# Weight pieces of a delta-rule kernel released at other moments, and step 1's scaled values computed on another engine

## The chip, the cores and the metric

The kernel runs on one core of a Trainium2 chip. Its time is the device time of one execution in microseconds (us). The engines are named as in the profile: PE (TensorE, with PEld for its weight loads), DVE (VectorE), ACT (ScalarE), POOL (GpSimd) and SP (SyncE, which issues most DMAs here).

## The reference

A delta-rule attention over 4 batches, 8 heads, 768 tokens of 48 dimensions, then a feed-forward block with a leaky slope per hidden unit; all in fp32.

```python
k_n = k / (np.linalg.norm(k, axis=-1, keepdims=True) + 1e-06)
for t in range(S):
    kt, vt, bt = (k_n[:, :, t], v[:, :, t], beta[:, :, t, None])
    y[:, :, t] = np.einsum('bhd,bhde->bhe', q[:, :, t], state)
    v_old = np.einsum('bhde,bhd->bhe', state, kt)
    state = state + bt[:, :, :, None] * np.einsum('bhd,bhe->bhde', kt, vt - v_old)
x = y.transpose(0, 2, 1, 3).reshape(B * S, H * D)      # 3072 x 384
h = x @ w_in                                           # 384 x 2048
g = np.maximum(h, 0.0) + alpha * np.minimum(h, 0.0)
out = g @ w_out                                        # 2048 x 384
```

## The kernel before

The sequence is cut into 12 chunks of 64 tokens, and each chunk into two steps of two batches (steps 0 to 23, two batches in the two halves of the partitions). Within a chunk the recurrence becomes a triangular system, which is solved with block inverses. The outputs of a chunk's two steps are transposed into `xt`, and the feed-forward block of that chunk (`ffn_in`, line 1075, then `ffn_out`) is woven between the attention matmuls of later steps. The whole schedule is written out by hand: the order of the program's text is the order on each engine's queue.

The start has a path of its own. `first_chunk` solves steps 0 and 1 together: DVE places the inverses (`place_small`, line 706), PE makes `matrix` and `own_values` for both steps, then three `rounds` follow (`one_round`, lines 857 and 912), whose third gives `u`. Then come `outputs` and `to_ffn`. `second_pair` does the same for steps 2 and 3 with pieces of `ffn_in(0)` in between (`alongside`). `scale_first` (line 845) multiplies a step's values by the norms of its keys: three products, for step 0 on POOL and for step 1 on DVE in `first_chunk`.

`busy` issues matmuls whose result nobody reads, between the start's real ones.

The weights arrive as raw 64-bit words (twice the bytes) and are converted in the kernel: `weights` handles them in pieces. A piece is fetched by one DMA on SP into a staging place (line 223), then ACT makes two passes (lines 240 and 242), DVE shifts (line 256), and POOL or DVE adds (line 263). `w_in` has 12 pieces of 512 KB and `w_out` 16 pieces of 384 KB; they are numbered from 0. The ids of a piece name its staging place; a place may be filled again once the piece in it was added. The staging places of `w_out`'s pieces 3 to 6 lie in the part of `w_out` itself that is filled last, which is free by then.

A DMA waits on SP, and with it everything behind it on SP, until the last writer and readers of its destination are done. `pause(n, upto)` (line 1671) writes one element of a staging place by a memset on POOL ahead of the fetch, so that the fetch can't start before POOL has come that far. Before the change it stands for `w_in`'s piece 4 (line 1671, ahead of the three rounds) and for piece 5 (in `second_pair`), and `pause_out` (line 1683) for `w_out`'s pieces 0 and 1. `w_out`'s pieces 3 and 4 are fetched in `second_pair` by `fetch_out(4)` and `fetch_out(5)`, and then one more piece behind each finished addition (the last argument of `weights`, `pace`, is 1). The additions of `w_out`'s first five pieces are on POOL, the others on DVE.

## Time and profile before

| | |
|---|---|
| three runs | 652.60, 651.75, 646.87 us; median 651.75 |
| the profiled execution | 648.95 us, of which the span from the first to the last instruction is 647.2 |
| mean granted clock of PE | 0.997 |
| PE / PEld busy | 635.0 / 562.7 us (98% / 87% of the span) |
| DVE / ACT / POOL busy | 482.9 / 258.6 / 125.3 us |
| DMA | 36.89 MB, of 106,799 packets 99,872 under 512 B |
| SP's wait for the memsets at line 1671 | 16.6 us in two waits |

The page has one row for each group of instructions with the same line, engine and tiles. In a timeline a row is a run of equal instructions: start in us from the span's start, how long they took, engine and line, what was written from what, shapes, count, and in brackets the idle time before them with what ended it. A row that names "issue" tells of time in which the engine waited for nothing that the profile shows. "SPq" rows are DMAs issued by SP; how long a transfer took to land is told apart from it.

### The profile page before, as it was taken

What the parts mean: (1) busy time and instruction counts of PE and PEld (TensorE: products, weight loads), DVE (VectorE), ACT (ScalarE), POOL (GpSimd) and SP (SyncE); (2) the same over time, 40 slices, a digit from 0 to 9 for tenths busy, and PEclk for the clock granted to TensorE, in tenths of its full rate; (3) what the DMA queues carried; (4) which work ended last, traced back from release to release, by engine and by line L of the source; (5) the groups of instructions that cost most, each with busy time, mean ns of one, the idle gap of its engine ahead of it and who ended that gap; (6) DMA issues with size and microseconds to landing.
All of it is one profiled execution on the core that took longest, in us unless ns stands there. A gap on an engine that the chain in (4) does not pass through costs nothing.

```text
span 647.2 us, 21391 instructions
## 1 busy us (share of the span) xinstructions
PE 635.0 (98%) x9177; PEld 562.7 (87%) x9177; DVE 482.9 (75%) x1160; ACT 258.6 (40%) x605; POOL 125.3 (19%) x248
## 2 busy tenths in 40 slices
PE   8899999999999999999999999999999999999997
PEld 7677787567889989989989989989999999999997
DVE  5858689978998788578678577678868568477383
ACT  6667664245553253254154144034045054042240
POOL 7267610010001000000000010000044053062360
PEclk9989999999999999999999999999999999999999
DMA  8668755113511320311210211211221210100000
GB/s 131 169 160 240 208 129 129 23 29 64 99 25 29 76 50 3 69 37 23 60 27 17 46 32 26 41 40 22 43 42 19 54 23 2 39 2 3 25 0 26
DMA packets 106799, 36.89 MB, mean 57 GB/s; under 512 B 99872, under 2 KB 103088, under 8 KB 106704
## 3 DMA queue, kind: packets, MB, share of 16 engines
q1 hardware_dynamic: 104832, 35.03, 25.0%
q8 instruction: 72, 1.18, 0.8%
q10 hardware_dynamic: 1872, 0.49, 0.4%
q14 instruction: 23, 0.19, 0.1%
HBM read 30.78 MB, written 4.72 MB: 55 GB/s over the span
## 4 chain that ended last, share of the span: by engine, by line
PE 86%; DVE 8%; issue 2%; ACT 2%; POOL 1%; DMA 1%; SPq 0%; POOLq 0%; DVEq 0%; ACTq 0%
PE p_ffn L1075 24%; PE p_ffn L1140 17%; PE p_more L1392 8%; PE p_more L1308 5%; PE p_ffn L1118 4%; PE p_ffn L1298 3%; PE p_ffn L1392 3%; PE p_ffn L1303 2%; PE p_pair L430 2%; PE p_pair L807 2%; PE p_pair L747 2%; PE p_pair L486 2%; PE p_pair L930 2%; PE p_pair L917 2%; PE p_pair L795 1%
## 5 line engine op out<-in xcount | busy, mean ns | idle before, releaser
L1075 PE MATMUL p_ffn<-xt,w_in 128*128 128x256 f32 x768 | 177.5, 384 | 0.7 <-DVE act L1087 0.5
L1075 PEld LDWEIGHTS p_ffn<-xt,w_in 128*128 128x128 f32 x768 | 142.0, 190 | 21.5 <-issue 1.5
L1085 ACT ACTIVATE act<-p_ffn 128x512 f32<-128x512 f32 x56 | 33.3, 595 | 80.4 <-PE p_ffn L1075 80.2
L1087 DVE SCALAR_TENSOR_TENSOR act<-act,al_t,p_ffn 128x256 f32<-128x256 f32 x112 | 48.5, 474 | 20.0 <-ACT act L1085 19.7
L1332 POOL TENSOR_TENSOR k_t<-k_t 128x128 f32<-128x128 f32 (+1 forms) x48 | 29.9, 623 | 167.5 <-ACT k_t L1327 165.0
L571 DVE TENSOR_TENSOR block<-block,prod 128x30 f32<-128x30 f32 (+9 forms) x150 | 50.0, 333 | 5.2
L565 DVE TENSOR_TENSOR prod<-block 128x30 f32<-128x30 f32 (+9 forms) x150 | 49.0, 327 | 4.2 <-POOL block L555 2.7
L419 POOL TENSOR_TENSOR beta_t<-beta_t,rec 128x8 f32<-128x8 f32 x20 | 5.1, 257 | 235.2 <-DVE rec L413 219.3
L1140 PE MATMUL p_ffn<-w_out,act 128*128 128x192 f32 x288 | 49.6, 328 | 0.0
L973 ACT COPY xt<-p_pair 128x384 f32<-128x384 f32 x22 | 10.4, 478 | 91.2 <-PE p_pair L969 77.5
L1140 PEld LDWEIGHTS p_ffn<-w_out,act 128*128 128x128 f32 x288 | 46.6, 190 | 0.3
L1332 POOL TENSOR_TENSOR block<-block 128x128 f32<-128x128 f32 (+1 forms) x48 | 28.0, 583 | 16.0 <-ACT block L1327 13.5
L1298 PE MATMUL p_ffn<-xt,w_in 128*128 128x256 f32 x96 | 28.7, 381 | 0.5 <-DVE o_sb L1160 0.5
L759 ACT COPY inv<-p_pair 32x256 f32<-32x256 f32 x40 | 14.5, 361 | 24.9 <-DVE u L921 24.1
L1160 DVE TENSOR_TENSOR o_sb<-u,p_ffn 128x192 f32<-128x192 f32 x24 | 7.9, 351 | 20.5 <-PE p_ffn L1140 20.0
L799 ACT COPY y<-p_pair 128x384 f32<-128x384 f32 x22 | 10.5, 479 | 31.1 <-PE p_pair L795 29.5
L1346 DVE SCALAR_TENSOR_TENSOR act<-block,al_t,act 128x256 f32<-128x256 f32 x32 | 19.1, 638 | 4.7 <-ACT block L1342 4.7
L1327 ACT COPY k_t<-p_more 128x512 f32<-128x512 f32 x16 | 9.4, 587 | 31.7 <-PE p_more L1308 27.9
L825 DVE TENSOR_TENSOR r<-v_raw,p_pair 64x192 f32<-64x192 f32 (+1 forms) x60 | 21.2, 353 | 1.0
L1392 PE MATMUL p_more<-w_out,act 128*128 128x192 f32 x128 | 21.9, 329 | 0.0
L1118 PE MATMUL p_ffn<-w_out,act 128*128 128x384 f32 x64 | 21.7, 490 | 0.0
L921 DVE TENSOR_TENSOR u<-p_pair,wgt 128x384 f32<-128x384 f32 x20 | 11.1, 555 | 14.0 <-PE p_pair L747 14.0
(286 smaller groups left out, 1424.1 us busy)
## 6 DMA issues: line engine op xcount, KB each, us to landing
v_raw<-in_v_dram SPq DMA_DIRECT2D x48, 96.0 KB, 3.1
qp<-in_q_dram SPq DMA_DIRECT2D x48, 96.0 KB, 3.1
out_dram<-o_sb SPq DMA_DIRECT2D x90, 48.0 KB, 1.6
space_out<-in_moe_w_out_dram SPq DMA_DIRECT2D x11, 384.0 KB, 4.0
ke<-in_k_dram SPq DMA_DIRECT2D x43, 96.0 KB, 3.4
kl<-in_k_dram SPq DMA_DIRECT2D x80, 48.0 KB, 2.7
w_out<-in_moe_w_in_dram SPq DMA_DIRECT2D x6, 512.0 KB, 5.1
w_out<-in_moe_w_out_dram SPq DMA_DIRECT2D x5, 384.0 KB, 5.9
```

The source lines that it names most:

```text
L565: nc.vector.tensor_tensor(out=prod, in0=r[:, 0:j, j : j + 1].to_broadcast([128, j, n]), in1=r[:, j : j + 1, j + 1 : HB].to_broadcast([128, ...
L571: nc.vector.tensor_tensor(out=r[:, 0:j, j + 1 : HB], in0=r[:, 0:j, j + 1 : HB], in1=prod, op=ALU.add)
L825: nc.vector.tensor_tensor(out=r[to, a], in0=v_in[to, a], in1=p[own, a, :, 0:D], op=ALU.subtract)
L1075: nc.tensor.matmul(p_h[:, i], w_in[:, t, (f + i) * 128 : (f + i + 1) * 128], xt[:, t], start=(t == 0), stop=(t == KT - 1),)
L1085: nc.scalar.activation(g, p_h, ACT.Relu, scale=-1.0)
L1087: nc.vector.scalar_tensor_tensor(out=g[:, i], in0=g[:, i], scalar=al_t[:, f + i : f + i + 1], in1=p_h[:, i], op0=ALU.mult, op1=ALU.add,)
L1118: nc.tensor.matmul(p_o[u], gs[f // 2][:, f % 2, u * 128 : (u + 1) * 128], w_out[:, f], start=(f == 0), stop=(f == FT - 1),)
L1140: nc.tensor.matmul(p, x(i), w(i), start=(i == 0), stop=(i == FP - 1))
L1298: nc.tensor.matmul(p[:, f * 256 : f * 256 + 256], w(2, f), xt[:, 2], start=True, stop=False)
L1308: nc.tensor.matmul(q[:, j], a, b, start=True, stop=True)
L1332: nc.gpsimd.tensor_tensor(out=dst, in0=a, in1=b, op=ALU.add)
L1392: nc.tensor.matmul(p, x(i), w(i), start=(i == 0), stop=(i == FP - 1))
```

## The change

Four edits. The values of step 1 are scaled by `scale_by_head`, twelve products on ACT, one for each head and half (128x48 or 64x48), four of them behind `slopes()` and eight ahead of `eliminate_small`; the three products on DVE in `first_chunk` go, and the last `busy` in front grows from 1.2 to 1.8 matmuls of 512 columns. In `first_chunk` the shift of `w_in`'s piece 1 stands between the two additions of the third round and its addition right behind them; `pause` for piece 4 stands behind that instead of ahead of the rounds. In `weights`, where there is a pace, each fetch behind an addition is preceded by a one-element memset into its staging place on the engine of that addition. In `second_pair`, `fetch_out(4)` becomes `pause_out(3, 4)`, and `fetch_out(5)` goes, so that piece 4 and all later ones are fetched one behind each addition, at first one addition later than before. In the built program the order of the DMAs on SP and of the matmuls on PE stays the same.

```diff
@@ weights, finish
                 while n < last and ids[n] not in ids[i + 1 : n]:
+                    if pace:
+                        engine.memset(stages[ids[n]][0:1, 0:1].bitcast(FP32), 0.0)
                     n += 1
                     fetch(n)
@@
+    def scale_by_head(n, which):
+
+        if n not in rhs_:
+            rhs_[n] = work.tile([128, 2, G, D], FP32, name="r")
+        x = v_raw[n].rearrange("p (g a) d -> p a g d", a=2)
+        w = stats[n][0].rearrange("p (g a) -> p a g", a=2)
+        for a, to, own in which:
+            for g in range(G):
+                nc.scalar.mul(rhs_[n][to, a, g], x[own, a, g], w[own, a, g : g + 1])
@@ first_chunk
         turn_matrix(0, nc.scalar)
-        scale_first(1, nc.vector)
         z_0 = own(0)
@@ first_chunk
         for n in both:
             mask(n)
+        for i in range(2):
+            rounds(i)
+        for x in [one_round(n, 2, ps_big()[:, :, 0:WY]) for n in both]:
+            now(x)
+            convert(1)
         pause(STAGED, STAGED + 1)
-        for i in range(3):
-            rounds(i)
-        convert(1)
         y_0 = outputs(0, ps_big()[:, :, 0:WY])
         now(y_0)
         begin_in()
-        convert(2)
+        convert(1)
         now(outputs(1, ps_big()[:, :, 0:WY]))
@@ the start
     slopes()
+    scale_by_head(1, [(0, slice(0, 128), slice(0, 128))])
     busy(3.2, ffn_banks[0])
@@ the start
-    busy(1.2, big[1][:, 0])
+    scale_by_head(1, [(1, half(0), half(1)), (1, half(1), half(0))])
+    v_raw.pop(1)
+    busy(1.8, big[1][:, 0])
     eliminate_small()
@@ second_pair
         alongside(2, 2)
-        fetch_out(4)
+        pause_out(3, 4)
         burst(lambda i, p: one_round(i, 1, p), G * D)
@@ second_pair
         burst(lambda i, p: one_round(i, 2, p), G * D)
-        fetch_out(5)
         alongside(3, 3, (part(blocks, 2), 2))
```

## The prediction

> **What bounds the kernel now.** I read the page first, then busy time by stage, then the timeline of each engine around the edits. On the page TensorE (PE) is busy for 98% of the span.

> ```profile
> span 647.2 us, 21391 instructions
> PE 635.0 (98%) x9177; PEld 562.7 (87%) x9177; DVE 482.9 (75%) x1160; ACT 258.6 (40%) x605; POOL 125.3 (19%) x248
> ...
> q8 instruction: 72, 1.18, 0.8%
> ```

> All edits act before 115 us. Busy time by stage (after the stretch: its length, then PE, PEld, DVE, ACT, POOL busy, clock, DMA share, GB/s) tells what there is to win:

> ```profile
> 26.97:33.68 6.71, 6.01 (x313) 5.34 (x313) 5.47 (x12) 5.44 (x12) 4.37 (x5) 1.00 0.05 16
> 33.68:34.67 0.99, 0.00 (x1) 0.00 (x1) 0.00 (x0) 0.55 (x1) 0.23 (x2) 1.00 0.00 0
> 34.67:38.34 3.67, 3.67 (x78) 3.13 (x78) 2.51 (x6) 1.53 (x3) 2.17 (x2) 0.54 0.54 147
> ...
> 60.00:69.25 9.25, 9.21 (x218) 7.09 (x211) 6.67 (x18) 5.33 (x12) 8.58 (x15) 1.00 0.96 270
> 69.25:70.23 0.98, 0.00 (x0) 0.00 (x0) 0.13 (x1) 0.00 (x0) 0.86 (x3) 1.00 1.02 389
> ...
> 80.00:105.00 25.00, 24.93 (x238) 20.74 (x237) 21.30 (x60) 14.20 (x33) 4.16 (x10) 1.00 0.60 140
> ```

> Until 34 us a serial chain runs (place the inverses, rounds); from 38 us PE is the bound. Two holes of 1 us stand out, at 33.68 and 69.25, and a stretch at clock 0.54. Both holes are "issue", PE waiting for nothing that the profile shows. Queue q8 moved 1.18 MB, which over PE's 18,354 instructions is 64 B each; its packets are 16 KB, so one holds 256 instructions, 128 pairs of load and matmul. The holes lie 765 matmuls apart, six times 127.5. I read them as PE running out of instructions. The trace's q8 packet for the first hole started at 31.70, 1.3 us after the count passed the boundary before (30.43), in an idle DMA; for the second it started at 67.97, 3.4 us after (64.60), in a DMA share of 0.96.

> ```profile
> 27.43 1.10 DVE L845 TENSOR_TENSOR r<-v_raw,first_norm 128x192 f32<-128x192 f32 x3
> 27.73 0.59 ACT L884 COPY act<-p_pair 128x512 f32<-128x512 f32 x1 [2.40 <-PE p_pair L857]
> 28.56 0.56 DVE L895 COPY act<-p_pair 128x384 f32<-128x384 f32 x1
> 35.19 0.56 DVE L912 TENSOR_TENSOR u<-act,p_pair 128x384 f32<-128x384 f32 x1 [1.70 <-PE p_pair L857]
> 36.16 3.21 POOL L263 TENSOR_TENSOR w_in<-w_out,w_in 128x512 uint32<-128x512 uint32 x2 [2.25 <-DVE w_out L256]
> 39.32 0.09 POOL L1671 MEMSET w_out<- 1x1 f32 x1
> ```

> **Part 1: step 1's values on ACT.** Three DVE products (1.10 us) leave. They stood between the inverses and the copy at 28.56, whose matmuls (started 27.48, 0.63 us) end at 28.11: DVE gains 0.4, the rest was hidden. The order of the built program puts twelve ACT products in. Nearest rows: 64x80 at 231 ns, 128x16 at 218, 64x16 at 180, 128x128 at 396; 48 columns lie near the first two, so 0.23 each. Four (0.9 us; bounds 0.7 to 1.6) fall into ACT's 1.60 us idle before 20.88; eight (1.8; 1.4 to 3.2) into the 2.40 before 27.73. Without that cover, or at the upper bound, 0.8 of it delays the copy at 27.73. The filler grows by 0.6 of 512 columns: 3.2 of them took 3.04 us, so 0.6 us within PE's 1.25 us wait before 26.97. **-0.4 us** (-0.5 to +0.4).

> **Part 2: a shift between two additions, fifth piece later.** The shift (L256, 0.4 us) enters the 1.70 us that DVE waits for the stalled matmuls before 35.19, so it costs nothing; without that wait, 0.4. POOL's two 1.6 us additions started at 36.16 because both shifts came after the second u; now the first starts when POOL is free of the masks (33.88) and ends near 35.2, the second near 37.4. The fifth w_in piece is released by a memset behind the first addition: 35.3 instead of 33.94. It took 3.8 us to land, so 39.1; ACT first reads it at 39.39. Nothing, with 0.3 us to spare. The sixth piece, at the head of a DMA stream that is saturated to 58 us, is released behind the second addition: 37.5 instead of 39.44. ACT waits for that stream (2.69 us idle before 43.89), but PE idles only 0.65 us in 50 to 60. **-0.3 us** (0 to -0.7).

> **Part 3: w_out's pieces one at a time.** Thirteen one-element memsets enter, each behind an addition, each holding one DMA: six on POOL (0.09 each by L1671), seven on DVE (0.06 by L279). DVE has 3.7 us idle from 80 to 105, which covers its 0.4. The SP order stays, but each held DMA now holds the queue. Pieces 3, 4, 5 (from 0) were issued at 64.28, 64.94, 65.43 and landed in 4.2 to 6.4 us, under each other; now they wait for POOL's additions that end at 67.74, 69.16, 71.18. A piece alone lands in 3.2 us, so at 71.0, 72.5, 74.5; ACT reads them at 72.39, 73.43, 74.49. Their traffic leaves the time in which PE's instructions were late, so I drop most of the hole:

> ```profile
> 70.23 0.56 PE L857 MATMUL p_pair<-r,sums 64*64 64x48 f32 x24 [0.98 <-issue]
> ```

> **-0.9** (0 to -1.0). PE then arrives 0.9 earlier and piece 5 is that much late for ACT; behind it wait the xt copies and the next Relu. Most fits into ACT's gaps: **+0.2** (0 to +1.2).

> [...]

> The dear place is later. Piece 9 was released by an addition on POOL, and SP issued it at 74.87; now it waits for the addition of piece 5 on DVE (82.79 to 83.3). Behind it on SP stand ten loads and piece 10:

> ```profile
> 74.87 0.33 SPq L223 DMA_DIRECT2D space_out<-in_moe_w_out_dram  x1
> 75.25 2.59 SPq L175 DMA_DIRECT2D kl<-in_k_dram  x4
> 77.88 1.43 SPq L137 DMA_DIRECT2D qp<-in_q_dram  x2
> 79.35 2.88 SPq L137 DMA_DIRECT2D v_raw<-in_v_dram  x4
> 86.14 0.34 SPq L223 DMA_DIRECT2D w_out<-in_moe_w_out_dram  x1
> ...
> 89.99 0.56 ACT L240 ACTIVATE w_out<-w_out 128x384 uint32<-128x384 uint32 x1
> 91.25 0.60 ACT L1085 ACTIVATE sums<-p_ffn 128x512 f32<-128x512 f32 x1 [0.70 <-PE p_ffn L1075]
> ...
> 95.37 0.60 ACT L1085 ACTIVATE sums<-p_ffn 128x512 f32<-128x512 f32 x1 [2.15 <-PE p_ffn L1075]
> ```

> In the times of before: memset 83.4, plus 0.35 + 2.59 + 1.43 + 2.88, gives piece 10 at 90.7 instead of 86.14. Rows near it landed in 3.3 to 4.6 us: 94.0 to 95.3, where ACT wants it at 89.99. ACT blocks, with the Relu of 91.25 behind it. That runs 0.55 later, then 0.60, then two DVE slopes (0.87): the bank is free at 96.0 to 97.3. PE fills the other bank until 95.3, so it stalls 0.7 to 2.0; near the middle, **+1.4** (0 to +2.0). By piece 13 SP has caught up (97.4 against 97.77), so it happens once.

> **Sum.** -0.4 - 0.3 - 0.9 + 0.2 + 1.4 = 0.0 against the profiled execution's own 648.95 us (span 647.2). The three runs had a median of 651.75, 2.8 above it. I forecast the middle of the two, **650.3 us**: no change.

> **Rivals.**
> *Slower: piece 10 is later still* (0.25). It decides once piece 10 lands after 93.3 (95.3 less 0.55, 0.60, 0.87). In the saturated stretch w_in pieces took 6.9 to 9.3 us; the ten loads just ahead speak for that, the DMA share of 0.60 against. Landing at 97.6 to 100.0 stalls PE 4.3 to 6.7 instead of 1.4: 653.2 to 655.6.
> *The pacing buys nothing* (0.15): earlier transfers and ke loads alone make the instructions late, the hole stays; the hole at 33.68 in an idle DMA speaks for it. 0.9 more: 651.2.
> *The clock* (0.15). From 34.69 the clock was 0.50 for 3.4 us, after a stretch with gaps. A longer filler might avoid it. Full-speed rows (outputs 1.08 us at 72.29 against 2.08 here, transposes 0.66 against 1.41) price it at -1.7: 648.6. Against: the hole at 33.68 stays. [...]

> **How the numbers follow.** The forecast holds 0.45. Nearly all of it, and most of the rivals, lie within 1% (6.5 us), about what a measurement of this kernel can tell from no change: the holes and the slow clock together are below 4 us. Faster by over 1% has 0.08, from the clock and a run that starts low (646.87); slower 0.15, from a stall at the far end with more behind it; same 0.77. The range goes from 646.0 (clock won and no stall make 647.2, less 1.2 for a low run) to 656.5 (the stall at its far end, 655.6, and the hole still there).

> **What would show it.** Right: the copy at 28.56 comes 0.4 earlier; the sixth piece is issued near 37.5; no hole near 69; SP issues piece 10 some 4 us later, and ACT waits for it with PE idle for 1 to 2 us near 95. Wrong: no wait of ACT there, or the holes as long as before, or a wait at 72 to 77 that stops PE.

## The result, and the profile after

The changed kernel took 655.02 us (median of 18 runs, 650.80 to 657.62), the kernel before 647.63 (18 runs, 645.93 to 652.60). The ratio is 1.009 (95% interval 1.0065 to 1.0115): by it the change makes the kernel 5.8 us slower (the two medians are 7.4 apart), where 650.3 and "no change" were forecast. Costs below go by the ratio.

The first lines of the page after stand beside those of before: a span of 655.9 us instead of 647.2, with the same work on PE and the same 1.18 MB of instructions.

```profile
span 655.9 us, 21415 instructions
PE 635.4 (97%) x9177; PEld 561.5 (86%) x9177; DVE 483.6 (74%) x1164; ACT 261.5 (40%) x617; POOL 124.7 (19%) x254
...
q8 instruction: 72, 1.18, 0.7%
```

PE's order is the same in both kernels, so the start of the same matmul tells where time was lost. Matmuls are counted from the start of the program; times are from the two profiled executions (that of after, 657.62 us, is the longest of its 18 runs, so it shows more loss than the median):

| matmul | before, us | after, us | after minus before |
|---|---|---|---|
| 400 | 28.82 | 28.87 | 0.0 |
| 892 | 48.40 | 49.86 | +1.5 |
| 1000 | 53.95 | 58.19 | +4.2 |
| 1200 | 62.97 | 67.78 | +4.8 |
| 1365 | 70.25 | 73.63 | +3.4 |
| 1490 | 79.57 | 84.23 | +4.7 |
| 1650 | 95.38 | 102.65 | +7.3 |
| 1700 | 100.09 | 108.86 | +8.8 |
| 9170 | 642.48 | 651.19 | +8.7 |

Two places hold nearly all of it: 42 to 61 us, where w_in's pieces arrive, and 95 to 107 us, where w_out's pieces 10 to 12 do. Behind matmul 1700 nothing changes any more.

The first place, in busy time by stage (after the stretch: its length, then PE, PEld, DVE, ACT, POOL busy, clock, DMA share, GB/s), with the stretch that answers to 80 to 105 of before as the last:

```profile
26.69:33.68 6.99, 5.68 (x314) 5.13 (x313) 4.25 (x10) 6.63 (x17) 4.58 (x5) 1.00 0.15 59
33.68:34.62 0.94, 0.23 (x17) 0.16 (x8) 0.36 (x2) 0.59 (x1) 0.50 (x1) 1.00 0.00 0
...
53.38:56.40 3.02, 0.21 (x11) 0.08 (x3) 1.10 (x3) 2.02 (x4) 0.52 (x2) 1.00 0.97 299
57.44:60.85 3.41, 3.41 (x69) 2.58 (x68) 2.16 (x6) 2.53 (x5) 2.41 (x4) 0.50 0.07 19
...
82.00:107.30 25.30, 20.68 (x213) 16.20 (x211) 17.95 (x53) 13.50 (x30) 3.54 (x8) 1.00 0.67 156
```

The start, with its hole at 33.68, is as it was. A hole of 3 us stands at 53.38, in a DMA share of 0.97, and 1 us behind it PE runs for 3.41 us at half its clock. The kernel before has no hole at these matmuls; its PE timeline has all 32 in one row:

```profile
52.11 0.85 PE L486 MATMUL p_pair<-k_t 48*64 48x64 f32 x32
```

In the last stretch PE is busy for 20.7 of 25.3 us, where it was busy for 24.93 of 25.

The timeline of POOL and of PE shows the release of the two w_in pieces (the memsets, L1684) and that the 3 us hole is "issue" (a row gives the idle time from the modelled end of the last matmul, 0.2 us less than from its start):

```profile
34.12 1.31 POOL L263 TENSOR_TENSOR w_in<-w_out,w_in 128x512 uint32<-128x512 uint32 x1 [0.82 <-DVE w_out L256]
35.36 0.09 POOL L1684 MEMSET w_out<- 1x1 f32 x1
35.97 1.29 POOL L263 TENSOR_TENSOR w_in<-w_out,w_in 128x512 uint32<-128x512 uint32 x1 [0.52 <-DVE w_out L256]
37.21 0.09 POOL L1684 MEMSET w_out<- 1x1 f32 x1
...
56.40 0.46 PE L488 MATMUL p_pair<-k_t 48*64 48x64 f32 x14 [2.81 <-issue]
```

The second place, first on SP. Piece 9 (the last of the three at 80.52, issued at 88.30) holds ten loads and piece 10:

```profile
80.52 8.10 SPq L223 DMA_DIRECT2D space_out<-in_moe_w_out_dram  x3
88.68 2.59 SPq L175 DMA_DIRECT2D kl<-in_k_dram  x4
91.32 1.29 SPq L137 DMA_DIRECT2D qp<-in_q_dram  x2
92.65 2.66 SPq L137 DMA_DIRECT2D v_raw<-in_v_dram  x4
95.43 0.56 SPq L223 DMA_DIRECT2D w_out<-in_moe_w_out_dram  x1
...
97.46 1.04 SPq L223 DMA_DIRECT2D space_out<-in_moe_w_out_dram  x2
```

Then on ACT, which waits for pieces 10 and 11, and on PE, which waits behind that for a bank (ffn_in is L1087 here, the Relu L1097):

```profile
100.28 0.55 ACT L240 ACTIVATE w_out<-w_out 128x384 uint32<-128x384 uint32 x1 [5.25 <-DMA w_out<-in_moe_w_out_dram]
100.73 0.58 ACT L1097 ACTIVATE sums<-p_ffn 128x512 f32<-128x512 f32 x1
...
103.46 0.56 ACT L240 ACTIVATE w_out<-space_out 128x384 uint32<-128x384 uint32 x1 [1.71 <-DMA space_out<-in_moe_w_out_dram]
```

```profile
83.39 0.67 PE L1087 MATMUL p_ffn<-xt,w_in 128*128 128x256 f32 x2 [0.72 <-ACT act L1097]
...
102.36 2.83 PE L1087 MATMUL p_ffn<-xt,w_in 128*128 128x256 f32 x12 [2.09 <-DVE sums L1099]
107.27 1.10 PE L1087 MATMUL p_ffn<-xt,w_in 128*128 128x256 f32 x4 [1.46 <-DVE sums L1099]
```

### The profile page after: what moved, and what is told of

Its sections match the earlier page's. It is cut to its first block, busy times and chain, and to the rows that moved or that the text cites. A ratio compares the mean times of both kernels' runs of the same rounds, so it can differ in the third digit from the quotient of the medians.

```text
span 655.9 us, 21415 instructions
## 1 busy us (share of the span) xinstructions
PE 635.4 (97%) x9177; PEld 561.5 (86%) x9177; DVE 483.6 (74%) x1164; ACT 261.5 (40%) x617; POOL 124.7 (19%) x254
## 3 DMA queue, kind: packets, MB, share of 16 engines
q8 instruction: 72, 1.18, 0.7%
## 4 chain that ended last, share of the span: by engine, by line
PE 84%; DVE 7%; ACT 2%; DMA 2%; issue 2%; SPq 1%; POOL 1%; ACTq 0%; DVEq 0%; POOLq 0%
PE p_ffn L1087 21%; PE p_ffn L1152 17%; PE p_more L1404 8%; PE p_more L1320 5%; PE p_ffn L1130 4%; PE p_ffn L1310 3%; PE p_ffn L1404 3%; PE p_ffn L1315 2%; PE p_pair L809 2%; PE p_pair L432 2%; PE p_pair L749 2%; PE p_pair L942 2%; PE p_pair L929 2%; PE p_pair L797 1%; PE p_pair L488 1%
## 5 line engine op out<-in xcount | busy, mean ns | idle before, releaser
L1087 PE MATMUL p_ffn<-xt,w_in 128*128 128x256 f32 x768 | 178.7, 385 | 5.2 <-DVE sums L1099 3.9
L1087 PEld LDWEIGHTS p_ffn<-xt,w_in 128*128 128x128 f32 x768 | 142.1, 190 | 26.8 <-ACT w_out L242 2.5
L1097 ACT ACTIVATE act<-p_ffn 128x512 f32<-128x512 f32 x56 | 33.3, 595 | 82.5 <-PE p_ffn L1087 82.2
L985 ACT COPY xt<-p_pair 128x384 f32<-128x384 f32 x22 | 10.4, 477 | 90.7 <-PE p_pair L981 76.9
L809 PE MATMUL p_pair<-beside,k_t 48*64 48x112 f32 x704 | 21.7, 259 | 1.1 <-issue 0.9
L966 DVE TENSOR_TENSOR beside<-beside,p_pair 48x384 f32<-48x384 f32 (+1 forms) x38 | 20.8, 549 | 2.1 <-PE p_pair L958 1.9
```

Of the source, the lines that this page charges most:

```text
L809: nc.tensor.matmul(p[half(t ^ a), a, g], k_t[n][dims(a), g, half(t)], beside[bp][dims(a), t, g])
L1087: nc.tensor.matmul(p_h[:, i], w_in[:, t, (f + i) * 128 : (f + i + 1) * 128], xt[:, t], start=(t == 0), stop=(t == KT - 1),)
L1097: nc.scalar.activation(g, p_h, ACT.Relu, scale=-1.0)
```

## The experiments

Each was timed beside the kernel before; the ratio is to that. Two more, `pages_moved` and `extra_traffic`, ran once each (653.94 and 650.66 us), for their profiles.

| kernel | median, us | before, us | ratio (95%) |
|---|---|---|---|
| only_scale | 647.58 | 647.66 | 0.9999 (0.9985 to 1.0014) |
| only_rounds | 649.50 | 647.66 | 1.0029 (1.0005 to 1.0052) |
| only_pace | 651.53 | 647.66 | 1.0063 (1.0046 to 1.0080) |
| nine_early | 650.54 | 647.66 | 1.0039 (1.0011 to 1.0067) |
| pace_memsets | 651.85 | 647.65 | 1.0061 (1.0046 to 1.0076) |
| shift_alone | 647.95 | 647.65 | 0.9999 (0.9981 to 1.0016) |
| fifth_alone | 649.30 | 647.65 | 1.0024 (1.0008 to 1.0040) |
| sixth_held | 647.65 | 647.65 | 1.0002 (0.9990 to 1.0013) |
| pace_nine | 647.65 | 647.42 | 1.0001 (0.9985 to 1.0017) |
| mended | 651.05 | 647.42 | 1.0060 (1.0039 to 1.0080) |
| no_scale | 649.01 | 647.80 | 1.0021 (1.0005 to 1.0037) |
| no_pacing | 648.48 | 647.80 | 1.0013 (0.9997 to 1.0028) |
| scale_pace | 649.79 | 647.80 | 1.0027 (1.0013 to 1.0042) |
| fifth_back | 647.21 | 647.80 | 1.0005 (0.9983 to 1.0027) |

### The parts by themselves

`only_scale` is the kernel before with step 1's values on ACT:

```diff
-        scale_first(1, nc.vector)
+    scale_by_head(1, [(0, slice(0, 128), slice(0, 128))])
     busy(3.2, ffn_banks[0])
...
-    busy(1.2, big[1][:, 0])
+    scale_by_head(1, [(1, half(0), half(1)), (1, half(1), half(0))])
+    busy(1.8, big[1][:, 0])
```

> Before, with step 1's values on ACT and the longer filler alone. Theory: the loss sits in the other two parts, so this lies within 0.2% of before, 0 to 0.4 us faster, with the copy of the first values some 0.4 us earlier. Rival: the early microseconds move the hand-off between PE and its instruction fetches for the whole start, and this alone is 3 us or more slower.

It changes nothing, as expected: the copy of the first values does come 0.4 us earlier (28.14 instead of 28.56). The hole at 69 us, which the prediction priced, is not in its profile though every release of a piece is as before: it is not there in every execution.

`only_rounds` is the kernel before with the shift between the additions and the fifth piece behind the last round:

```diff
-        pause(STAGED, STAGED + 1)
-        for i in range(3):
+        for i in range(2):
             rounds(i)
-        convert(1)
+        for x in [one_round(n, 2, ps_big()[:, :, 0:WY]) for n in both]:
+            now(x)
+            convert(1)
+        pause(STAGED, STAGED + 1)
...
-        convert(2)
+        convert(1)
```

> Before, with the shift between two additions and the fifth w_in piece behind the last round alone. Theory: the saturated stream of w_in pieces starts some 2 us earlier, PE's instruction packets come later in it, and PE has holes of 1 to 3 us between 47 and 58 us at matmul counts 853 and 981: 3 to 5 us slower. Rival: those holes in the profile of the changed kernel were chance or belong to the pacing, and this lies within 1 us of before.

It costs 1.9 us (0.3 to 3.4), less than the 3 to 5 expected. Its trace shows the fifth piece (piece 4, counted from 0) issued at 35.53 (33.94 before) and the sixth at 37.59 (39.44 before): 2.1 us apart instead of 5.5, and the sixth takes 6.1 us to land instead of 4.4. In its timeline and its stages a hole of 1.5 us at matmul 725, in a DMA share of 0.90, is followed by half the clock; another of 1.5 us stands at 980. At 853, where one was expected, there is none:

```profile
41.44 0.81 PE L946 MATMUL p_pair<-u,kl 64*64 64x48 f32 x18 [1.51 <-issue]
```

```profile
41.55:44.96 3.41, 3.41 (x24) 2.39 (x24) 1.35 (x3) 1.20 (x3) 1.19 (x1) 0.50 1.11 218
```

`only_pace` is the kernel before with w_out's pieces let go one at a time:

```diff
+                    if pace:
+                        engine.memset(stages[ids[n]][0:1, 0:1].bitcast(FP32), 0.0)
...
-        fetch_out(4)
+        pause_out(3, 4)
...
-        fetch_out(5)
```

> Before, with w_out's pieces let go one at a time alone. Theory: piece 9 holds SP until the addition of piece 5 on DVE, piece 10 lands some 5 us late, ACT blocks with the Relu behind it, and PE stalls 2 to 4 us between 94 and 106; the hole at 69 goes (0.9 to 1.0): together 1.5 to 3 us slower. Rival: ACT's wait is hidden by the other bank, and this is 0 to 1 us faster.

It costs 4.1 us, more than the 1.5 to 3 expected, with three waits of PE in its timeline where the prediction had one near 95:

```profile
78.38 0.67 PE L1077 MATMUL p_ffn<-xt,w_in 128*128 128x256 f32 x2 [1.08 <-ACT act L1087]
...
96.31 2.83 PE L1077 MATMUL p_ffn<-xt,w_in 128*128 128x256 f32 x12 [1.04 <-DVE sums L1089]
101.22 3.04 PE L1077 MATMUL p_ffn<-xt,w_in 128*128 128x256 f32 x13 [1.45 <-DVE sums L1089]
```

### The held ninth piece

`pace_memsets` is the kernel before with the memsets alone, `fetch_out(4)` and `fetch_out(5)` kept:

```diff
+                    if pace:
+                        engine.memset(stages[ids[n]][0:1, 0:1].bitcast(FP32), 0.0)
```

> Before, with the memsets behind each addition alone: w_out's pieces 3 and 4 are fetched as before, and every later piece one addition earlier than in the pacing edit, so piece 9 waits for POOL's addition of piece 4 and not for DVE's of piece 5. Theory: the cost of the pacing edit is the one piece fewer under way; the memsets alone cost nothing, within 0.7 us of before, and no stall of PE near 78, 95 and 100 us. Rival: the waits that the memsets make cost by themselves, 2 us or more over before.

My expectation fell: 4.0 us stay. `fetch_out(5)` does nothing, because by then the addition of piece 0 has fetched the piece itself; so removing it moves no fetch ("at first one addition later" in the section on the change was a misreading, and so is piece 4 fetched by `fetch_out(5)` in the section on the kernel before). With or without it, piece 9 follows DVE's addition of piece 5 (issued at 83.46 here, 83.29 in `only_pace`).

`nine_early` is the kernel after, with piece 9 let go together with piece 8, behind POOL's addition of piece 4:

```diff
-                last = min(count, limit or count, n + pace if pace else count)
+                last = min(count, limit or count, n + pace + (i == 4) if pace else count)
```

> The changed kernel, with w_out's piece 9 let go together with piece 8, behind the addition of piece 4 on POOL, instead of behind that of piece 5 on DVE. Theory: SP passes the ten loads 5 us earlier, piece 10 lands before ACT wants it, the stalls of PE near 100 and 106 go: 3 to 4 us faster than the changed kernel, so 2 to 3 us slower than before. Rival: the stall comes from the one-at-a-time release itself, not from what stands behind piece 9 on SP; then it stays within 1 us of the changed kernel.

The ratio falls from 1.009 to 1.0039, some 3.3 us, and the two waits near 95 and 100 are gone from its trace. `pace_nine` makes the same edit to `pace_memsets`:

> The kernel before, with the memsets in `weights`, and piece 9 of w_out let go together with piece 8, behind POOL's addition of piece 4, so that only pieces 10 and on wait for DVE. The memsets alone cost 4.1 us. Theory: all of that comes from one held DMA, piece 9's, which keeps the ten loads behind it and piece 10 on SP for 4 us. Then piece 10 is issued near 86, PE has no stall near 95 and near 100, and the time lies within 0.7 us of the kernel before, the most being left for ACT's wait for piece 5 near 76. Rival: the memsets and the late pieces 3 to 8 cost by themselves; then 2 to 4 us stay.

Nothing of the 4.0 us is left. Its SP timeline has piece 9 at 76.25 with pieces 7 and 8, the loads right behind it, and piece 10 at 84.58 (90.59 in `pace_memsets`):

```profile
74.65 1.93 SPq L223 DMA_DIRECT2D space_out<-in_moe_w_out_dram  x3
76.63 2.59 SPq L175 DMA_DIRECT2D kl<-in_k_dram  x4
...
84.58 0.34 SPq L223 DMA_DIRECT2D w_out<-in_moe_w_out_dram  x1
```

So the price of the pacing is one held DMA at the head of SP's queue; the twelve memsets of this kernel and the later pieces 4 to 8 cost nothing that was measured (piece 3 is fetched as before in it). By the start of the same matmuls, the two waits near 95 and 100 are 2.8 us of `pace_memsets` (1.35 + 1.49) and of `only_pace` (1.28 + 1.49). The rest of the 4 us differs between those two profiles: 1.2 at matmul 1485 in `only_pace` (ACT waits for piece 5), 2.2 at matmul 891 in `pace_memsets` (ACT waits for a w_in piece, ahead of anything that its edit touches).

### The fifth and sixth pieces of w_in

`shift_alone` has the shift between the additions, with `pause` for the fifth piece where it was; `fifth_alone` has the rounds as before, with `pause` behind them; `sixth_held` is `only_rounds` with the sixth piece let go from DVE, behind the first new state:

```diff
# fifth_alone, against the kernel before
-        pause(STAGED, STAGED + 1)
         for i in range(3):
             rounds(i)
-        convert(1)
+        convert(2)
+        pause(STAGED, STAGED + 1)
...
-        convert(2)
+        convert(1)
# sixth_held, against only_rounds
-        pause(STAGED + 1, STAGED + 2)
+        nc.vector.memset(in_stages[STAGED + 1][0:1, 0:1].bitcast(FP32), 0.0)
+        fetch_in(STAGED + 2)
```

> Before, with the shift of piece 1 between the two additions of the last round, and its addition right behind, but the fifth w_in piece let go ahead of the rounds as before. Theory A (the sixth piece and the stream behind it start 2 us earlier, and PE's instruction packets come late in that stream): as slow as both edits together, 1 to 3 us over before, with holes near matmul counts 853 and 981. Theory B (the fifth piece's own transfer, moved under the fetch that PE asks for at matmul 598, is what comes in its way): within 0.7 us of before, no hole at 725.

> Before, with the fifth w_in piece let go behind POOL's addition of piece 1, the shift staying behind both additions: the piece is issued near 38 us instead of 34, the sixth near 39.5 as before. Theory A: the stream starts as before, so only ACT's wait for the fifth piece counts (it wants it at 39.4, it lands near 42): 0 to 1 us slower, no new holes. Theory B: a hole of 1 us or more at matmul count 725 or 853, 1 to 3 us slower.

> Both edits of the rounds, with the sixth w_in piece held to its old time (near 39.5 to 40.5 instead of 37.4) by a memset on DVE behind the first new state. Theory A: the stream starts as late as before, and the 1.8 us of the two edits go: within 0.7 us of before. Theory B: the hole at 725 stays, 1 to 2 us over before.

| kernel | fifth piece issued, landed | sixth piece issued, landed | cost by the ratio |
|---|---|---|---|
| before | 33.94, 37.73 | 39.44, 43.81 | |
| shift_alone | 33.46, 37.17 | 36.87, 40.95 | 0.0 us |
| sixth_held | 35.93, 39.84 | 38.90, 44.18 | +0.1 us |
| only_rounds | 35.53, 39.78 | 37.59, 43.72 | +1.9 us |
| fifth_alone | 37.59, 41.55 | 39.30, 46.64 | +1.6 us |

Neither theory holds by itself: the times of `shift_alone` and `fifth_alone` fit B (though `fifth_alone` has no hole at 725 or 853), that of `sixth_held` fits A. By these five kernels the shift is free, and an earlier sixth piece too, as long as the fifth is let go early. What goes with a cost is a fifth piece that no longer uses the empty DMA of 34 to 38 us (a share of 0.00 from 33.68 to 34.67 in the kernel before, and of 0.21 from 33.7 to 40 in `fifth_alone`, whose fifth piece comes at 37.59) and then flows together with the sixth (issued 1.7 and 2.1 us apart in the two dear kernels, 3.0 to 5.5 in the others). How it costs differs: in `only_rounds` by holes ("issue"), in `fifth_alone` by a wait for ACT, as ACT's timeline, PE's timeline and the stage behind show:

```profile
46.72 0.68 ACT L240 ACTIVATE w_in<-w_out 128x512 uint32<-128x512 uint32 x1 [3.30 <-DMA w_out<-in_moe_w_in_dram]
```

```profile
50.93 2.04 PE L1075 MATMUL p_ffn<-xt,w_in 128*128 128x256 f32 x4 [3.69 <-ACT w_in L240]
```

```profile
48.79:59.03 10.24, 8.10 (x105) 6.22 (x106) 8.68 (x19) 6.82 (x16) 6.83 (x13) 0.50 0.95 261
```

PE waits 3.7 us for ACT, which waits for the sixth piece, and half the clock follows for 10.24 us, three times 3.41. (This profiled execution, 652.52 us, is its kernel's longest; the median lost 1.6.) A wait there does not settle the matter, though: `sixth_held`, which costs nothing, has one as well:

```profile
48.47 1.10 PE L1075 MATMUL p_ffn<-xt,w_in 128*128 128x256 f32 x4 [1.49 <-ACT w_in L240]
```

And the profile of `shift_alone`, which costs nothing by its median, has a hole of 1.9 us at matmul 980 with half the clock for 6.83 us at it.

### Are the holes PE's instructions?

`pages_moved` is the kernel before with the last filler of the start replaced by very small ones, 60 more matmuls in all:

```diff
-    busy(1.2, big[1][:, 0])
+    short(32, big[1][:, 0])
```

> The kernel before with its last filler, 1.2 matmuls of 512 columns, replaced by 32 very small pairs of matmuls: some 60 more instructions pairs on PE, ahead of the holes. Theory: PE's holes of about 1 us fall where a packet of 256 instructions ends, so at the same count from the start (470, 598, 725 and so on, 127.5 apart), which is 60 matmuls earlier in the program than before. Rival: they belong to a place of the program, and then they move to counts 60 higher (530, 658, 785). One look; the time itself tells little.

The holes of its PE timeline lie at matmuls 470, 598 and 725, the counts of the other kernels, and so 60 matmuls earlier in the program:

```profile
31.24 0.26 PE L857 MATMUL p_pair<-r,inv 64*64 64x48 f32 x2 [1.01 <-issue]
...
35.66 0.26 PE L857 MATMUL p_pair<-act 64*64 64x48 f32 x2 [1.23 <-issue]
...
40.28 0.32 PE L930 MATMUL p_pair<-u,a_t 64*64 64x48 f32 x4 [1.54 <-issue]
```

`extra_traffic` is the kernel before with 2 MB more to move behind the first four pieces of w_in:

```diff
+    for i in range(6, 10):
+        nc.sync.dma_start(out=in_stages[i], in_=moe_w_in[0:128, 0:W_IN_P].bitcast(U32))
```

> The kernel before with four more loads of 512 KB each, into the staging places of pieces 6 to 9, issued behind the first four pieces of w_in, so that the DMA engines are busy from about 28 to 37 us where they were idle before. What is loaded is not used. Theory: the packet of PE's instructions that is asked for near 27.8 or 30.4 us then comes 1 to 3 us later than in an idle DMA, and the hole at matmul 470 or 598 is 2 to 4 us instead of 1. The fifth w_in piece is late too, which costs by itself. Rival: instructions do not wait for other traffic; the hole stays at 1.0 us.

The hole at matmul 470 is 3 us, as predicted, in a DMA share of 0.87; the packet of instructions that ended last ahead of PE's going on moved at 31.17 to 32.21, 1.27 us before it, where in the kernel before the packet had moved at 28.37 to 29.24. PE's timeline, then the stage:

```profile
33.48 2.16 PE L857 MATMUL p_pair<-act 64*64 64x48 f32 x71 [3.03 <-issue]
```

```profile
30.20:33.50 3.30, 0.27 (x22) 0.14 (x13) 0.22 (x1) 3.16 (x7) 3.30 (x3) 1.00 0.87 345
```

Over the 18 profiles of this case there are 30 holes of more than 0.8 us, from the start of one matmul to the start of the next, at a packet's end past matmul 400. In every one PE goes on 1.2 to 1.7 us (median 1.41) after a packet on q8 has ended. In an idle DMA (shares of 0.01 to 0.07) one turn recurs to the hundredth: 3.73 us from PE's passing one packet's end to its going on behind the next, at matmul 598 in seven profiles. PE itself took 2.80 us from one end to the other (30.88 to 33.68 in after); the difference is the hole of 0.93. In two more profiles that turn was 4.00 us, in `pages_moved` 4.4. In the holes with loads under way (shares of 0.38 to 1.08) the turn was 4.6 to 8.1 us (7.66 for the 3 us hole of after).

### What the parts cost together

`mended` is the kernel after with piece 9 let go early, `fetch_out(4)` in the place of `pause_out(3, 4)`, and the sixth piece let go from DVE as in `sixth_held`:

> The kernel after with three places changed: piece 9 of w_out let go with piece 8; `fetch_out(4)` as in the kernel before instead of `pause_out(3, 4)`; the sixth piece of w_in let go by a memset on DVE, behind the first new state, instead of on POOL. Theory: the held piece 9 and the fifth and sixth w_in pieces going back to back are all of the 6 us that the change costs. Then the time is within 0.7 us of the kernel before. Rival: something else is left, such as ACT's products or the pacing of pieces 3 to 8; then 1.5 to 3 us stay.

3.9 us stay, though each mended part alone cost nothing. So I took its three parts in pairs (`no_scale`, `no_pacing`, `scale_pace`: `mended` without the scaling, without the edits to w_out's pieces, without the edits to the rounds and w_in), and made `fifth_back`: `mended` with both releases of w_in's pieces as before (`fetch_out(5)`, which does nothing, is back too):

```diff
# fifth_back, against mended
+        pause(STAGED, STAGED + 1)
         for i in range(2):
             rounds(i)
         for x in [one_round(n, 2, ps_big()[:, :, 0:WY]) for n in both]:
             now(x)
             convert(1)
-        pause(STAGED, STAGED + 1)
...
-        nc.vector.memset(in_stages[STAGED + 1][0:1, 0:1].bitcast(FP32), 0.0)
-        fetch_in(STAGED + 2)
+        pause(STAGED + 1, STAGED + 2)
```

> The version `mended` without its edit of step 1's values: the three products on DVE and the shorter filler of the kernel before; the shift between two additions, the fifth piece behind the last round, the sixth let go from DVE, the memsets of w_out with piece 9 let go early all stay. Theory A: the 3.6 us that `mended` still cost come from the scaling on ACT together with the later fifth piece; then this is within 0.9 us of the kernel before. Theory B: they come from the later pieces of w_in and of w_out together, with no part of the scaling; then 2.5 to 4 us stay.

> The version `mended` without any edit of w_out's pieces: scaling on ACT, the shift, the fifth piece behind the last round, the sixth let go from DVE. Theory A (scaling and later fifth piece together): 2.5 to 4 us stay. Theory B (pieces of w_in and w_out together): within 0.9 us of the kernel before.

> The kernel before with the scaling on ACT and the memsets of w_out, piece 9 let go early; the rounds and w_in's pieces as in the kernel before. Both parts cost nothing alone. Theories A and B both put it within 0.9 us of the kernel before. A third, C, that the scaling and the paced w_out pieces cost together, has 2.5 to 4 us here.

> As `scale_pace`, with the shift between two additions too: all four edits of the change, with the fifth piece let go ahead of the rounds as in the kernel before and piece 9 let go early. Theories A and B: the fifth piece has the idle DMA of 34 to 38 us again, nothing is left, and it is within 0.9 us of the kernel before. Rival: 2.5 us or more stay, from the starts of the sixth piece or from the scaling with the shift.

None of the three theories on pairs holds: the pairs lose 1.4, 0.8 and 1.7 us by their ratios (the middle one's interval includes zero), not 3 in one and none in the others. But `fifth_back` is at 1.0005 (-1.1 to +1.7 us): no cost of the scaling, the shift and the memsets together was measured once w_in's pieces are let go as before and piece 9 early. Against `mended` that is 3.6 us by the ratios, by two releases alone (the two were timed on two chips, each beside the kernel before). `scale_pace`, which is `fifth_back` without the shift, loses 1.7 us (0.8 to 2.7); the two intervals overlap, so a cost of about 1 us in both is not excluded. Nor is the distance of the fifth and sixth pieces all of it: in `mended` they are issued at 35.99 and 39.44, as far apart as in the kernels that cost nothing. Why `sixth_held` is free by itself and not in `mended` stays open. In all these kernels the holes and the stretches at half the clock fall differently from profile to profile: `fifth_back` alone spreads from 645.98 to 653.50. No version came out measurably ahead of the kernel before.

## Why the prediction was wrong, point by point

**The scaling (-0.4).** Measured 0.0 (0.9999). The copy came 0.4 us earlier, as predicted, but the end does not hang on it. The holes at packet ends behind it (0.97 and 0.93 us from start to start in `only_scale`) are the likely reason; no run tests that.

**The shift and the fifth piece (-0.3, 0 to -0.7).** This step failed. The issue times were nearly right: 35.5 for the fifth piece (predicted 35.3), 37.3 for the sixth (37.5). The fault was to give the step no loss at all: "nothing, with 0.3 us to spare" for the fifth piece, and for the sixth only the gain of an earlier stream. The two pieces now share the DMA: in after the fifth took 5.1 us to land instead of 3.8 and the sixth 6.0 instead of 4.4, so that the fifth landed 2.8 us later (40.56 against 37.73) and the sixth, issued 2.1 us earlier, only 0.5 us earlier (43.28 against 43.81). `only_rounds` measured +1.9, and `mended` against `fifth_back` 3.6. That the releases cost this is measured; by which wait they do is not settled, as `sixth_held` and `mended` show.

**The hole at 69 (-0.9).** Failed. It is gone in after, but also in `only_scale`; and it is in `no_scale`, with paced pieces (0.98 us, to 69.10); of the 18 profiles only that one and before have it. A hole of one profiled execution was booked as a property of the kernel. That these holes are waits for PE's instructions agrees with `pages_moved` (holes at matmuls 470, 598 and 725 with 60 matmuls more ahead of them) and `extra_traffic` (3.03 us in a DMA share of 0.87); what was missing is that such holes can come with the change as well: after has holes of 1.2, 1.2 and 3.0 us (from start to start) at 40 to 56 us, where before has none. Its DMA share from 34 to 50 us is 0.84 instead of 0.75; that this difference delayed the packets is argued from `extra_traffic`, not tested. The rival "the pacing buys nothing" had instructions made late by other traffic, but only at 69 us. In after the packet for matmul 598 moved at 31.92 to 33.20, while PE ran until 33.68, and PE went on at 34.61. Over the 18 profiles the 30 holes of 0.9 to 3.3 us stand at some 1,240 packet ends (69 past matmul 400 in each).

**Piece 5 late for ACT (+0.2, 0 to +1.2).** At the far end of its range: +1.2 at matmul 1485 in `only_pace`, +0.9 in after. ACT waited 0.80 and 1.23 us for pieces 4 and 5 in after and could not make it up, since the xt copies that PE wants stand behind (at 80.59 in after, right behind its read of piece 5 at 80.13).

**Piece 10 (+1.4, 0 to +2.0, "happens once").** The mechanism was right, and its times within 0.3 us: `only_pace` issued piece 9 at 83.29 (predicted 83.4) and piece 10 at 90.41 (90.7), ACT waited and PE stalled. "Once" was wrong. Pieces 11 and 12 stand right behind piece 10 and were issued at 92.44 and 93.11; they landed in 5.4 and 6.0 us, so a second wait of 1.5 us followed the first of 1.3. The prediction looked only for when SP catches up, not for when the pieces land. The two cost 2.8 us against 1.4; with piece 9 let go early (`pace_nine`) they are gone.

**The sum and the base.** The parts measured alone give 0.0 + 1.9 + 4.1 = 6.0; by the ratio the change costs 5.8, the medians differ by 7.4. That the parts add up so well is partly luck: `mended` costs 3.9 though each of its parts cost nothing alone. The base was wrong by 2.7: I took the middle between the profiled 648.95 and the median 651.75 of three runs, and 18 runs have 647.63. That error went the other way, so that the forecast missed 655.02 by 4.7 only; and that 655.02 lies within 646.0 to 656.5 is luck too, as that end was one long stall at piece 10 with the hole at 69, on the high base.

**The signs.** Those named for being right came true: the copy came earlier (27.98 in after), the sixth piece was issued at 37.33, no hole stood near 69, piece 10 was issued 4.3 us later in `only_pace`, with ACT and PE waiting behind it. One named for being wrong came too, if later than 72 to 77: the wait at 78.38 in `only_pace`. Signs of the terms that were priced say nothing of a loss that was given no term.

**The rivals.** "Piece 10 is later still" gave 653.2 to 655.6 and so holds the measured median, but not by its mechanism: piece 10 itself landed in 3.7 us in `only_pace` and 4.8 in after, not in 7 to 9. "The clock" had a gain of 1.7 us, but the change went the other way: the mean granted clock of its 18 runs is 0.9960, that of the 110 runs of the kernel before beside the experiments 0.9975, which by an estimate (0.0015 of 650 us) is 1 us lost. In the profile of after the stretch at half the clock behind the holes is 57.44 to 60.85, 3.41 us as in `only_rounds`; in `fifth_alone` it is 10.24. What sets such a stretch off, or ends it, no run tests.

## What to carry to other kernels

A wait put ahead of a DMA was here a wait for everything behind it on that queue (in `only_pace` SP issued piece 9 at 83.29 instead of 74.87, and piece 10, ten loads behind it, at 90.41 instead of 86.14): before a release is moved, list what follows on the queue and when those transfers land, not only when they are issued, and keep such a wait off a late engine. Do not price the delay of an early transfer at nothing because it still lands in time by its old duration: here two that followed each other took 5.1 and 6.0 us to land instead of 3.8 and 4.4. Price a hole seen in one execution only after a second profile of the same kernel has shown it.
